# Two-level seven-product matrix multiplication: the last stage without GpSimd arithmetic, sums added by accumulating transfers

## The chip, the core and the metric

One core of one Trainium2 chip runs the kernel. The metric is the device time of the whole program in microseconds; the time of the kernel before is the median of three runs.

## The reference, cut to what matters

```python
X = np.fft.rfft(x, axis=1)                 # x: 8 x 3008 x 256, float32
Yr = Xr @ w_r - Xi @ w_i + b_r             # and Yi alike, then a soft threshold of 0.01
y = np.fft.irfft(Yr + 1j * Yi, n=3008, axis=1)

xt = y.transpose(0, 2, 1)
h = np.maximum(xt @ w_tok1, 0.0) @ w_tok2  # token mixing, 3008 -> 256 -> 3008
u = y + h.transpose(0, 2, 1)
h2 = np.maximum(u @ w_ch1, 0.0) @ w_ch2    # channel mixing, 256 -> 1536 -> 256
return u + h2
```

The last stage of the kernel computes the last two lines for units 2 to 4 (six of the eight batches): `u`, the two channel products with a ReLU between them, and `u + h2`.

## The kernel before, in words

The spectral part and the first two batches run first, up to about 1212 us of the span; the change leaves them alone. Then `channel7` takes over for the remaining tokens, in 17 chunks `n` of up to 1024 tokens. A chunk is cut into two halves of h = 512 tokens (448 or 490 in three of them), and the 256 channels into two blocks of 128, so `u` is a 2 x 2 block matrix `uf`. Both channel products are made with a seven-product scheme (P1 to P7 in place of eight block products). Every number is split into a high and a low part, so each product is three matmuls (`pinned`, line 1059): high x high, high x low, low x high.

`first7(n, g)` makes the hidden blocks of one group g (two groups of `TRIO` = 3 pairs of hidden blocks). For each pair it makes seven products into three PSUM banks: `x`, `w` and `q`. In order: P1 into x, copied by ScalarE (line 1076) to the block `c11`; P5 into w, copied to `c22` (1079); P6 added onto x, copied to `r12` (1082); P2 into q, added by VectorE to `c11` (1085); P7 added onto x, added by VectorE to `c22` (1088); P3 added onto w, added to `r12` by VectorE (1091), ReLU by ScalarE (1092); P4 added onto x, ReLU by ScalarE into `r21` (1095). The sequence P7, P3, P4 matters below: P4 adds into bank x, so it can't start until VectorE has read x after P7. The banks come from a pool of four.

`second7(n, g, ...)` makes the second channel product of group g, 21 products: results r = 0 to 6, three pairs k each, accumulated in one of three PSUM banks (`wc["sbanks"]`). `prepare(j, slot)` makes the moving operand of product j five steps ahead (`LEAD`): for r = 1, 2, 4, 6 VectorE first combines hidden blocks (lines 1122, 1124, 1126, 1128), then ScalarE makes the high part `rh` (1130 or 1133), then the low part `rl` is a subtraction: on VectorE for r = 0 and 5 (1131), and at line 1135 on GpSimd (`G`), but for three of the fifteen on VectorE. `product(j)` runs the three matmuls and fetches the weights of result r + 2 (`weights2`, line 1100, on SP's DMA queue, three buffers). When a result has its third pair, VectorE adds it to its block of `uf` (line 1147: seven such sums a group, r = 0 and r = 3 going to the same block); in the second group `store7` (line 1160) then stores finished blocks from SP's queue.

`channel7` interleaves them: one step is one first product and, from the second group on, `step()`: one second product of the group before, 21 steps behind, and one `prepare`. A step is thus six matmuls. Between steps stand the token mixing of the next chunk (`make_parts`, lines 1059 and 873, into bank `pu`; 37 sets of two halves), the block sums of its u (`sum_u`, lines 1037 to 1040) and its splits (`split_u7`, lines 150 and 153). TensorE's order is that of the program; the other queues are ordered ahead of time by a planner from its model of when each operand is ready, so an operation may stand earlier or later there than in the text. Every queue runs strictly in its order on the chip.

Of the kernel before, what the change touches and what calls it, by code (L numbers as in the profile page):

```python
# [11 lines left out]
F32 = mybir.dt.float32  # L12
F32R = mybir.dt.float32r
U32 = mybir.dt.uint32
AF = mybir.ActivationFunctionType
ALU = mybir.AluOpType
# [16 lines left out]
CW = 512  # L33
# [4 lines left out]
CW7 = 2 * CW  # L38
TRIO = 3
LEAD = 5  # L40
AT = (0, 3, 4, 1, 5, 6, 2)
SLOW = 1.75
SPECTRAL = 70.3 + NG * (SLOW - 0.7)
# [86 lines left out]
def tile_kernel(ctx: ExitStack, tc: tile.TileContext, io):  # L130
    nc = tc.nc
    V, S, G, PE, DMA, PUT = nc.vector, nc.scalar, nc.gpsimd, nc.tensor, nc.sync, nc.scalar
# [12 lines left out]
    def bank(name):  # L145
        return ps.tile([128, 512], F32, tag="w", name=name)
# [883 lines left out]
    def sum_u(n):  # L1030
        cw = chunks[n][2]
        h = cw // 2
        uf = ufs.pop(n)
        b11, b12, b21, b22 = (uf[:, t, k * h:(k + 1) * h] for t in range(2) for k in range(2))
        t = wc["seven"].tile([128, 4, CW], F32, tag="t7", name="t7", bufs=1)
        t1, t2, t3, t4_ = (t[:, k, :h] for k in range(4))
        V.tensor_tensor(out=t1, in0=b12, in1=b11, op=ALU.subtract)
        V.tensor_tensor(out=t2, in0=b22, in1=t1, op=ALU.subtract)
        V.tensor_tensor(out=t3, in0=b22, in1=b12, op=ALU.subtract)
        V.tensor_tensor(out=t4_, in0=b21, in1=t2, op=ALU.subtract)  # L1040
        us[n] = uf, (b11, t1, t2, b21, t3, b22, t4_), []

    def split_u7(n, i):
        h = chunks[n][2] // 2
# [12 lines left out]
    def pinned(out, wh, wl, xh, xl, start):  # L1057
        for n, (w, x) in enumerate(((wh, xh), (wh, xl), (wl, xh))):
            m = PE.matmul(out, lhsT=w, rhs=x, start=start and n == 0, stop=n == 2, skip_group_check=True)  # L1059
            tc.keep_in_program_order(m)  # L1060

    def first7(n, g):
        h = chunks[n][2] // 2
        ubs = us[n][2]
        blocks = [wc["tail"].tile([128, TRIO, CW], F32, tag="blk", name=k, bufs=8) for k in ("c11", "c22", "r12", "r21")]
        yield blocks
        for k in range(TRIO):
            p = TRIO * g + k
            c11, c22, r12, r21 = (t[:, k, :h] for t in blocks)
            x, w, q = (bank(name)[:, :h] for name in ("sx", "sw", "sq"))  # L1070

            def product(out, a, i, start):
                pinned(out, *left(p, a), ubs[i][:, 0, :h], ubs[i][:, 1, :h], start)

            product(x, 4, 0, True)
            S.copy(out=c11, in_=x)  # L1076
            yield
            product(w, 0, 1, True)
            S.copy(out=c22, in_=w)
            yield  # L1080
            product(x, 1, 2, False)
            S.copy(out=r12, in_=x)
            yield
            product(q, 5, 3, True)
            V.tensor_tensor(out=c11, in0=q, in1=c11, op=ALU.add)
            yield
            product(x, 2, 4, False)
            V.tensor_tensor(out=c22, in0=x, in1=c22, op=ALU.add)  # L1088
            yield
            product(w, 3, 5, False)  # L1090
            V.tensor_tensor(out=r12, in0=w, in1=r12, op=ALU.add)
            S.activation(out=r12, in_=r12, func=AF.Relu)
            yield
            product(x, 6, 6, False)
            S.activation(out=r21, in_=x, func=AF.Relu)
            yield

    def weights2(g, r):
        a = wc["seven"].tile([128, TRIO, 2, 128], F32R, name="a2s", bufs=3)
# [3 lines left out]
    def second7(n, g, blocks, odd):  # L1103
        h = chunks[n][2] // 2
        uf = us[n][0]
        banks = wc["sbanks"]
        x, w, q = (banks[i][:, :h] for i in ((2, 1, 0) if odd else (0, 1, 2)))
        outs = (x, w, x, q, x, w, x)
        homes = ((0, 0), (1, 1), (0, 1), (0, 0), (1, 1), (0, 1), (1, 0))
        weights, ready = {}, {}  # L1110

        def fetch(r):
            if r < 7:
                weights[r] = weights2(g, r)

        def prepare(j, slot):
            r, k = divmod(j, TRIO)
            hi, lo = (wc[name][:, slot, :h] for name in ("rh", "rl"))
            a, b, c, d = (t[:, k, :h] for t in blocks)
            src = (a, a, a, d, c, b, a)[r]  # L1120
            if r == 1:
                V.scalar_tensor_tensor(out=a, in0=a, scalar=0.0, in1=c, op0=ALU.max, op1=ALU.subtract)
            if r == 2:
                V.scalar_tensor_tensor(out=a, in0=b, scalar=0.0, in1=a, op0=ALU.max, op1=ALU.add)  # L1124
            if r == 4:
                V.scalar_tensor_tensor(out=c, in0=b, scalar=0.0, in1=c, op0=ALU.max, op1=ALU.subtract)
            if r == 6:
                V.tensor_tensor(out=a, in0=d, in1=a, op=ALU.subtract)  # L1128
            if r in (0, 5):
                S.activation(out=hi, in_=src, func=AF.Relu)  # L1130
                V.scalar_tensor_tensor(out=lo, in0=src, scalar=0.0, in1=hi.bitcast(F32), op0=ALU.max, op1=ALU.subtract)  # L1131
            else:
                S.copy(out=hi, in_=src)  # L1133
                eng = V if k == 0 and 2 <= r <= 4 else G
                eng.tensor_tensor(out=lo, in0=src, in1=hi.bitcast(F32), op=ALU.subtract)  # L1135
            ready[j] = hi, lo

        def product(j):
            r, k = divmod(j, TRIO)
            if k == 0:  # L1140
                fetch(r + 2)
            hi, lo = ready.pop(j)
            pinned(outs[r], weights[r][:, k, 0], weights[r][:, k, 1], hi, lo, r in (0, 1, 3) and k == 0)
            if k == TRIO - 1:
                i, j = homes[r]
                o = uf[:, i, j * h:(j + 1) * h]
                V.tensor_tensor(out=o, in0=outs[r], in1=o, op=ALU.add)  # L1147
                if g == 1 and r >= 3:
                    store7(n, i, j)

        return SimpleNamespace(prepare=prepare, product=product, fetch=fetch)

# [22 lines left out]
    def channel7(ns):  # L1175
        channels.close()
        wc["tail"] = ctx.enter_context(tc.tile_pool(name="tail", bufs=1, reuse_waits="tile"))
        for name, old in (("rh", "w2h"), ("rl", "w2l")):
            wc[name] = const.tile([128, 2 * TRIO, CW], F32R, tag=old, name=name)
        sums.close()  # L1180
        ps3 = ctx.enter_context(tc.tile_pool(name="ps3", bufs=1, space=bass.MemoryType.PSUM, reuse_waits="tile"))
        wc["sbanks"] = [ps3.tile([128, 512], F32, name=f"s{i}") for i in range(3)]
        wc["pu"] = ps3.tile([128, 512], F32, name="pu")
        seconds, count = [], [-7 * TRIO]

        def step():
            j = count[0]
            count[0] += 1
            if j >= 0:
                seconds[j // 21].product(j % 21)  # L1190
                if j % 21 in (19, 20) and j // 21 + 1 < len(seconds):
                    seconds[j // 21 + 1].fetch(j % 21 - 19)
            j += LEAD
            if 0 <= j < 21 * len(seconds):
                seconds[j // 21].prepare(j % 21, j % 6)

        for n in ns:
            after = n + 1 if n + 1 < len(chunks) else None
            mine = list(needs[after]) if after else []
            makes = {}  # L1200
            for i, g in enumerate(mine):
                m = make_parts(g)
                first = 1 + 6 * i if n == ns[0] else 22 - 9 * (len(mine) - 1 - i)
                makes[first], makes[first + (3 if n == ns[0] else 4)] = (m, i), (m, i)
            for g in range(2):
                f = first7(n, g)
                blocks = next(f)
                seconds.append(second7(n, g, blocks, len(seconds) % 2))
                if len(seconds) == 1:
                    for r in range(2):  # L1210
                        seconds[0].fetch(r)
                for t in range(7 * TRIO):
                    at = 7 * TRIO * g + t
                    next(f)
                    step()
                    if at in makes:
                        m, i = makes[at]
                        if next(m, None) is not None and i + 1 < len(mine):
                            load_wt2(mine[i + 1])
                            load_b2(mine[i + 1])  # L1220
                    if at == 33:
                        load_ahead(n + 2)
                    if after:
                        if at == 30:
                            sum_u(after)
                        if at in (32, 34):
                            split_u7(after, at // 2 - 16)
                        if at >= 37:
                            split_u7(after, at - 35)
        for _ in range(7 * TRIO):  # L1230
            step()

# [88 lines left out]
```

## Time and profile of the kernel before

| | us |
|---|---|
| median of three runs | 2477.83 (2476.95 to 2484.16) |
| the profiled execution | 2493.84 |
| its span, first to last instruction | 2492.1 |
| TensorE, busy | 2364.7 (95%) |
| VectorE, busy | 1843.5 (74%) |
| ScalarE, busy | 1336.6 (54%) |
| GpSimd, busy | 855.0 (34%) |

A busy time adds up the records of an engine's instructions. Records of neighbours overlap: matmuls are pipelined, and a VectorE or ScalarE instruction starts shortly before the one ahead of it has ended. So a busy share is not a share of the engine's own pace, and where pace matters the starts of neighbours are compared. The span has stages with different limits; the last one, from 1212 to 2488 us, is half of it.

### The profile page before, as it was taken

Reading aid. Unit: us, or ns where it says so; the run is one execution under the profiler, and the core shown is the slowest. Engines: PE = TensorE matmul, PEld = TensorE weight load, DVE = VectorE, ACT = ScalarE, POOL = GpSimd, SP = SyncE. Lnnn points to the kernel's source line nnn. Section 1 sums busy time; section 2 is a strip of 40 time slices with the busy share of each in tenths; the row PEclk is TensorE's granted clock in tenths of the full one; section 3 lists DMA queues with packets and bytes.
Section 4 is the critical chain, followed back from the end, with each engine's and each line's share of the span. In section 5 each row is a group of like instructions: output and inputs, shape, how many; then the busy total and the mean of one; then the engine's idle time right before and its main releaser. Section 6 shows DMA issues by size and latency. Waiting matters only on the chain.

```text
span 2492.1 us, 33718 instructions
## 1 busy us (share of the span) xinstructions
PE 2364.7 (95%) x12236; PEld 2032.4 (82%) x12236; DVE 1843.5 (74%) x2650; ACT 1336.6 (54%) x2419; POOL 855.0 (34%) x631
## 2 busy tenths in 40 slices
PE   8999999999999999999999999999999999998998
PEld 7778989999878888999787777887777778777776
DVE  7975667655656665554489888888888888988888
ACT  6754445444444443333466665666665566565665
POOL 0000332222222321221045444444444444444455
PEclk9999999999999999999999999999999999999998
DMA  8875577656466645434434444444444344453323
GB/s 213 259 239 168 161 238 216 184 168 195 139 193 185 179 147 190 142 119 135 153 114 127 129 146 135 135 136 125 136 127 143 111 132 132 130 162 114 117 89 97
DMA packets 196723, 383.73 MB, mean 154 GB/s; under 512 B 15893, under 2 KB 109677, under 8 KB 196557
## 3 DMA queue, kind: packets, MB, share of 16 engines
q1 hardware_dynamic: 162169, 314.98, 42.4%
q10 hardware_dynamic: 34388, 66.60, 8.0%
q8 instruction: 97, 1.59, 0.3%
q14 instruction: 69, 0.57, 0.1%
HBM read 274.30 MB, written 107.22 MB: 153 GB/s over the span
## 4 chain that ended last, share of the span: by engine, by line
PE 53%; DVE 30%; ACT 7%; DMA 4%; issue 3%; POOL 2%; SPq 1%; ACTq 0%; POOLq 0%; DVEq 0%
PE s L1059 6%; PE sx L1059 4%; DVE c L1124 4%; PE pu L873 3%; DVE rl L1131 3%; DVE c L1128 3%; PE ph L200 2%; PE px L488 2%; DVE ub L153 2%; PE po L201 2%; PE ph L202 2%; PE ph L201 2%; PE po L202 2%; DVE uf L1147 2%; PE po L200 2%
## 5 line engine op out<-in xcount | busy, mean ns | idle before, releaser
L1135 POOL TENSOR_TENSOR rl<-c,rh 128x512 fp32r<-128x512 f32 (+2 forms) x272 | 395.0, 1457 | 612.8 <-ACT rh L1133 523.6
L1059 PE MATMUL s<-rh,a2s 128*128 128x512 f32 (+2 forms) x1428 | 561.5, 396 | 0.1
L1059 PEld LDWEIGHTS s<-rh,a2s 128*128 128x128 f32 x1428 | 276.1, 193 | 56.7 <-ACT rh L1133 0.7
L1059 PE MATMUL s<-rl,a2s 128*128 128x512 f32 (+2 forms) x714 | 283.4, 397 | 5.6 <-POOL rl L1135 5.6
L1133 ACT CAST rh<-c 128x512 fp32r<-128x512 f32 (+2 forms) x306 | 187.2, 613 | 142.2 <-DVE c L1124 50.5
L1059 PE MATMUL sx<-ub,w 128*128 128x512 f32 (+2 forms) x612 | 193.8, 428 | 73.3 <-DVE c L1088 73.1
L1135 POOL TENSOR_TENSOR rl<-r,rh 128x512 fp32r<-128x512 f32 (+2 forms) x136 | 204.8, 1519 | 118.8 <-ACT rh L1133 109.5
L1059 PEld LDWEIGHTS sx<-ub,w 128*128 128x128 f32 x612 | 117.0, 203 | 116.9 <-DVE c L1088 97.8
L1131 DVE SCALAR_TENSOR_TENSOR rl<-c,rh 128x512 fp32r<-128x512 f32 (+2 forms) x204 | 165.4, 815 | 51.9 <-ACT rh L1130 51.5
L153 POOL TENSOR_TENSOR yl<-z,yh 128x512 fp32r<-128x512 f32 x72 | 96.1, 1335 | 301.9 <-ACT yh L150 301.8
L1147 DVE TENSOR_TENSOR uf<-s,uf 128x512 f32<-128x512 f32 (+2 forms) x238 | 159.5, 670 | 42.0 <-PE s L1059 42.0
L1059 PE MATMUL sx<-ub,ws 128*128 128x512 f32 (+2 forms) x612 | 177.1, 398 | 6.2 <-ACT c L1076 5.8
L914 DVE SCALAR_TENSOR_TENSOR hlo<-ph,hh 128x512 fp32r<-128x512 f32 (+4 forms) x180 | 113.9, 636 | 90.3 <-ACT hh L913 89.2
L913 ACT ACTIVATE hh<-ph 128x512 fp32r<-128x512 f32 (+4 forms) x180 | 100.1, 558 | 136.2 <-PE ph L202 131.4
L1130 ACT ACTIVATE rh<-c 128x512 fp32r<-128x512 f32 (+2 forms) x204 | 128.4, 630 | 82.6 <-PE s L1059 41.1
L1059 PE MATMUL sw<-ub,ws 128*128 128x512 f32 (+2 forms) x612 | 172.3, 390 | 0.0
L491 POOL TENSOR_TENSOR xf<-xf 128x256 f32<-128x256 f32 x84 | 72.9, 868 | 281.4 <-ACT xf L490 246.1
L1059 PEld LDWEIGHTS s<-rl,a2s 128*128 128x128 f32 x714 | 137.9, 193 | 36.2 <-POOL rl L1135 8.4
L153 DVE TENSOR_TENSOR xtl<-xf,xth 128x768 fp32r<-128x768 f32 x84 | 85.6, 1019 | 109.9 <-ACT xth L150 109.8
L200 PE MATMUL pm<-wmh,xth 128*128 128x256 f32 x504 | 146.3, 291 | 8.6 <-ACT xth L150 6.6
L201 PE MATMUL pm<-wml,xth 128*128 128x256 f32 x504 | 143.2, 284 | 0.0
L202 PE MATMUL pm<-wmh,xtl 128*128 128x256 f32 x504 | 143.0, 285 | 0.0
(185 smaller groups left out, 6171.5 us busy)
## 6 DMA issues: line engine op xcount, KB each, us to landing
a2s<-a_d SPq DMA_DIRECT2D x238, 384.0 KB, 3.0
wt<-wt_d SPq DMA_DIRECT2D x28, 940.0 KB, 5.8
x<-in_x SPq DMA_DIRECT2D x39, 480.0 KB, 4.6
wt<-ws_d SPq DMA_DIRECT2D x36, 512.0 KB, 3.7
a<-a_d SPq DMA_DIRECT2D x36, 512.0 KB, 5.0
b_d<-bt ACTq DMA_DIRECT2D x36, 512.0 KB, 4.7
a_d<-a ACTq DMA_DIRECT2D x36, 480.0 KB, 4.7
wt<-wt_d SPq DMA_DIRECT2D x21, 752.0 KB, 6.0
```

What stands on the lines that cost most here:

```text
L153: lo_eng.tensor_tensor(out=lo, in0=src, in1=hi.bitcast(F32), op=ALU.subtract)
L200: PE.matmul(out, lhsT=wh, rhs=xh, start=start, stop=False, skip_group_check=more)
L201: PE.matmul(out, lhsT=wh, rhs=xl, start=False, stop=False, skip_group_check=more)
L202: PE.matmul(out, lhsT=wl, rhs=xh, start=False, stop=stop, skip_group_check=more)
L913: S.activation(out=hh, in_=pt, func=AF.Relu)
L914: V.scalar_tensor_tensor(out=hlo, in0=pt, scalar=0.0, in1=hh.bitcast(F32), op0=ALU.max, op1=ALU.subtract)
L1059: m = PE.matmul(out, lhsT=w, rhs=x, start=start and n == 0, stop=n == 2, skip_group_check=True)
L1130: S.activation(out=hi, in_=src, func=AF.Relu)
L1131: V.scalar_tensor_tensor(out=lo, in0=src, scalar=0.0, in1=hi.bitcast(F32), op0=ALU.max, op1=ALU.subtract)
L1133: S.copy(out=hi, in_=src)
L1135: eng.tensor_tensor(out=lo, in0=src, in1=hi.bitcast(F32), op=ALU.subtract)
L1147: V.tensor_tensor(out=o, in0=outs[r], in1=o, op=ALU.add)
```

## The change

In the first products, P1 is copied by ScalarE from bank x into bank q (a bank of its own, `fq`, kept through the stage), P2 is accumulated onto it by TensorE, and ScalarE takes the ReLU of the sum straight into block `c11`: VectorE's addition of line 1085 is gone. So that TensorE adds onto what ScalarE wrote, `accumulator` runs one matmul over the bank at the start. The order becomes P1, P5, P4 of the pair before, P6, P2, P3, P7; P4 is thus deferred behind the next pair's P1 and P5. With `fq` kept, three banks of the pool are left for x and w. Blocks are tiles of one pair each, in 18 buffers.

In the second products, r = 0 is copied by ScalarE into the bank in which r = 3 then accumulates, so six sums a group are left. Each is copied by ScalarE to a staging tile (`st`, four buffers), and a DMA issued from GpSimd's queue adds it to the block of `uf` in SBUF (`accum_op`). All low parts are made by VectorE. The splits of the next chunk's u are one or two steps earlier in part.

```diff
+ADD = "dma"
...
-            product(x, 4, 0, True)
-            S.copy(out=c11, in_=x)
...
+            def p1():
+                nonlocal x
+                x = bank("sx")[:, :h]
+                product(x, p, 4, 0, True)
+                S.copy(out=q, in_=x)
...
+            def p2():
+                product(q, p, 5, 3, False)
+                S.activation(out=block(0, k), in_=q, func=AF.Relu)
...
+            def p7():
+                product(x, p, 2, 5, False)
+                c22 = blocks[1][k]
+                V.tensor_tensor(out=c22, in0=x, in1=c22, op=ALU.add)
+
+            def p4():
+                product(x, p, 6, 6, False)
+                S.activation(out=block(3, k), in_=x, func=AF.Relu)
+
+            return p1, p5, p4, p6, p2, p3, p7
...
-            if r in (0, 5):
+            if r == 5:
...
-                S.copy(out=hi, in_=src)
-                eng = V if k == 0 and 2 <= r <= 4 else G
-                eng.tensor_tensor(out=lo, in0=src, in1=hi.bitcast(F32), op=ALU.subtract)
+                split(hi, lo, src, S, V)
...
-                V.tensor_tensor(out=o, in0=outs[r], in1=o, op=ALU.add)
-                if g == 1 and r >= 3:
-                    store7(n, i, j)
+                if r == 0:
+                    S.copy(out=q, in_=x)
+                else:
+                    add(r)
+
+        def add(r):
+            i, j = homes[r]
+            o = uf[:, i, j * h:(j + 1) * h]
+            if ADD == "dma":
+                t = wc["tail"].tile([128, CW], F32, tag="st", name="st", bufs=4)[:, :h]
+                S.copy(out=t, in_=outs[r])
+                G.dma_start(out=o, in_=t, accum_op=ALU.add)
...
+            if g == 1 and r >= 3:
+                store7(n, i, j)
...
-                    next(f)
+                    k, i = divmod(t, 7)
+                    if i != 2:
+                        pairs[k][i]()
+                    elif last4:
+                        last4()
+                    if i == 2:
+                        last4 = pairs[k][2]
                     step()
```

## Rows read from the trace of the kernel before

**Rows 1.** Busy time by stretch, last stage: PE, PEld, DVE, ACT, POOL, clock, DMA, GB/s

```profile
1212.00:2488.00 1276.00, 1187.54 (x5404) 979.85 (x5402) 1086.35 (x1434) 770.54 (x1436) 597.02 (x408) 0.97 0.42 126
```

**Rows 2.** The products' line 1059: idle before it (us, times), by what ended it

```profile
  DVE c L1088: 171.0, 126
  ACT c L1076: 16.2, 22
  POOL rl L1135: 14.0, 14
```

**Rows 3.** Chain that ended last, in order of time: start, length in us, what

```profile
1214.19 1.03 PE pu L1059 x6
1215.22 0.88 PE pu L873 x8
...
1748.31 0.68 PE s L1059 x3
...
1750.35 1.28 PE pu L1059 x6
1751.63 1.09 PE pu L873 x10
```

**Rows 4.** Last stage by line and shape: count, busy us, mean ns, idle before

```profile
L1135 POOL TENSOR_TENSOR rl<-c,rh 128x512 fp32r<-128x512 f32 x224 | 330.9, 1482 | 448.1 <-ACT rh L1133 361.8 <-DVE c L1088 73.8 <-DVE r L1126 11.8
L1131 DVE SCALAR_TENSOR_TENSOR rl<-c,rh 128x512 fp32r<-128x512 f32 x168 | 135.7, 812 | 43.5 <-ACT rh L1130 43.1
L1124 DVE SCALAR_TENSOR_TENSOR c<-c,c 128x512 f32<-128x512 f32 x84 | 103.7, 1250 | 20.7 <-POOL rl L1135 20.7
L1128 DVE TENSOR_TENSOR c<-r,c 128x512 f32<-128x512 f32 x84 | 84.0, 1027 | 7.9 <-POOL rl L1135 7.9
L1126 DVE SCALAR_TENSOR_TENSOR r<-c,r 128x512 f32<-128x512 f32 x84 | 80.9, 990 | 0.1
L1085 DVE TENSOR_TENSOR c<-sq,c 128x512 f32<-128x512 f32 x84 | 57.1, 680 | 0.0
L1135 DVE TENSOR_TENSOR rl<-r,rh 128x512 fp32r<-128x512 f32 x56 | 52.2, 932 | 0.0
```

**Rows 5.** VectorE and GpSimd in order of time: start, length in us

```profile
1779.31 0.67 DVE L1131 SCALAR_TENSOR_TENSOR rl<-c,rh 128x512 fp32r<-128x512 f32 x1
1779.91 0.68 DVE L1088 TENSOR_TENSOR c<-sx,c 128x512 f32<-128x512 f32 x1
...
1781.63 1.30 POOL L1135 TENSOR_TENSOR rl<-c,rh 128x512 fp32r<-128x512 f32 x1 [3.40 <-ACT rh L1133]
...
1781.71 1.77 DVE L1131 SCALAR_TENSOR_TENSOR rl<-c,rh 128x512 fp32r<-128x512 f32 x1
```

**Rows 6.** ScalarE in order of time: first and last of twelve without a pause

```profile
1782.36 0.58 ACT L1095 ACTIVATE r<-sx 128x512 f32<-128x512 f32 x1
...
1787.90 0.64 ACT L150 CAST ub<-uf 128x512 fp32r<-128x512 f32 x1
```

**Rows 7.** Who waited for whom in the last stage: total us, times, longest

```profile
ACT r L1092 <- DVE r L1091: 128.6, 66, 4.0
...
DVE rl L1131 <- ACT rh L1130: 51.5, 49, 1.7
```

**Rows 8.** Stores (line 1160), then weight fetches (1100): issue ns, landing; SP's queue

```profile
L1160 SPq DMA_DIRECT2D out<-uf x74: 332/338/867, 1296.9 to 2489.1; - x74
DMA to landing us min/median/max: 1.4/2.6/6.5
...
L1100 SPq DMA_DIRECT2D a2s<-a_d x238: 319/320/542, 1193.2 to 2478.2; - x119
DMA to landing us min/median/max: 2.7/3.0/6.8
...
1775.22 38.61 SPq L1100 DMA_DIRECT2D a2s<-a_d  x9
```

**Rows 9.** The end of the chain: start, length in us, what

```profile
2483.08 3.21 POOL rl L1135 x2
...
2488.36 0.69 DVE uf L1147
```

More of the change, by code (lines that the diff above doesn't have):

```diff
@@ L1040, in sum_u @@
         V.tensor_tensor(out=t4_, in0=b21, in1=t2, op=ALU.subtract)
-        us[n] = uf, (b11, t1, t2, b21, t3, b22, t4_), []
+        us[n] = uf, (b11, t1, t2, b21, b22, t3, t4_), []
     def split_u7(n, i):
@@ L1060, in pinned, with accumulator @@
             tc.keep_in_program_order(m)
+    def accumulator(t):
+        w = wc["w1"][:, 0, 0]
+        tc.keep_in_program_order(PE.matmul(t, lhsT=w[:, :128], rhs=w[:, :CW], start=True, stop=True))
     def first7(n, g):
@@ L1064, in first7 @@
         ubs = us[n][2]
-        blocks = [wc["tail"].tile([128, TRIO, CW], F32, tag="blk", name=k, bufs=8) for k in ("c11", "c22", "r12", "r21")]
-        yield blocks
-        for k in range(TRIO):
-            p = TRIO * g + k
[L1069 to L1073, printed above, removed]
-            product(x, 4, 0, True)
-            S.copy(out=c11, in_=x)
[L1077 to L1096, printed above, removed]
@@ new lines, in first7, with block, product, pair @@
+        blocks = [[None] * TRIO for _ in range(4)]
+        steps = []
+        def block(i, k):
+            blocks[i][k] = wc["tail"].tile([128, CW], F32, tag="blk", name=("c11", "c22", "r12", "r21")[i], bufs=18)[:, :h]
+            return blocks[i][k]
+        def product(out, p, a, i, start):
+            pinned(out, *left(p, a), ubs[i][:, 0, :h], ubs[i][:, 1, :h], start)
+        def pair(k):
+            p = TRIO * g + k
+            x, w = None, None
+            q = wc["fq"][:, :h]
+            def p1():
[3 more added lines that the diff above has]
+                S.copy(out=q, in_=x)
+            def p5():
+                nonlocal w
+                w = bank("sw")[:, :h]
+                product(w, p, 0, 1, True)
+                S.copy(out=block(1, k), in_=w)
+            def p6():
+                product(x, p, 1, 2, False)
+                S.copy(out=block(2, k), in_=x)
+            def p2():
+                product(q, p, 5, 3, False)
+                S.activation(out=block(0, k), in_=q, func=AF.Relu)
+            def p3():
+                product(w, p, 3, 4, False)
+                r12 = blocks[2][k]
+                V.tensor_tensor(out=r12, in0=w, in1=r12, op=ALU.add)
+                S.activation(out=r12, in_=r12, func=AF.Relu)
+            def p7():
[6 more added lines that the diff above has]
+            return p1, p5, p4, p6, p2, p3, p7
@@ L1098, in weights2 @@
+        return [pair(k) for k in range(TRIO)], blocks
     def weights2(g, r):
@@ L1106, in second7 @@
         banks = wc["sbanks"]
-        x, w, q = (banks[i][:, :h] for i in ((2, 1, 0) if odd else (0, 1, 2)))
+        x, w = (t[:, :h] for t in (banks[:2], banks[1::-1])[odd])
+        q = banks[2][:, :h]
         outs = (x, w, x, q, x, w, x)
-        homes = ((0, 0), (1, 1), (0, 1), (0, 0), (1, 1), (0, 1), (1, 0))
+        homes = (None, (1, 1), (0, 1), (0, 0), (1, 1), (0, 1), (1, 0))
         weights, ready = {}, {}
@@ L1118, in prepare @@
             hi, lo = (wc[name][:, slot, :h] for name in ("rh", "rl"))
-            a, b, c, d = (t[:, k, :h] for t in blocks)
+            a, b, c, d = (t[k] for t in blocks)
             src = (a, a, a, d, c, b, a)[r]
             if r == 1:
-                V.scalar_tensor_tensor(out=a, in0=a, scalar=0.0, in1=c, op0=ALU.max, op1=ALU.subtract)
+                V.tensor_tensor(out=a, in0=a, in1=c, op=ALU.subtract)
             if r == 2:
@@ L1142, in product @@
             hi, lo = ready.pop(j)
-            pinned(outs[r], weights[r][:, k, 0], weights[r][:, k, 1], hi, lo, r in (0, 1, 3) and k == 0)
+            pinned(outs[r], weights[r][:, k, 0], weights[r][:, k, 1], hi, lo, r < 2 and k == 0)
             if k == TRIO - 1:
-                i, j = homes[r]
-                o = uf[:, i, j * h:(j + 1) * h]
+                if r == 0:
[9 more added lines that the diff above has]
+                G.dma_start(out=o, in_=t, accum_op=ALU.add)
+            else:
                 V.tensor_tensor(out=o, in0=outs[r], in1=o, op=ALU.add)
-                if g == 1 and r >= 3:
-                    store7(n, i, j)
+            if g == 1 and r >= 3:
+                store7(n, i, j)
         return SimpleNamespace(prepare=prepare, product=product, fetch=fetch)
@@ L1183, in channel7 @@
         wc["pu"] = ps3.tile([128, 512], F32, name="pu")
+        wc["fq"] = bank("fq")
+        accumulator(wc["fq"])
         seconds, count = [], [-7 * TRIO]
@@ L1187, in step @@
             j = count[0]
+            if j == 0:
+                accumulator(wc["sbanks"][2])
             count[0] += 1
@@ L1195, in step @@
                 seconds[j // 21].prepare(j % 21, j % 6)
+        last4 = None
         for n in ns:
@@ L1205, in channel7 @@
             for g in range(2):
-                f = first7(n, g)
-                blocks = next(f)
+                pairs, blocks = first7(n, g)
                 seconds.append(second7(n, g, blocks, len(seconds) % 2))
@@ L1227, in channel7 @@
                             split_u7(after, at // 2 - 16)
-                        if at >= 37:
-                            split_u7(after, at - 35)
+                        if at in (36, 37, 39, 40, 41):
+                            split_u7(after, {36: 2, 37: 3, 39: 4, 40: 5, 41: 6}[at])
+        last4()
         for _ in range(7 * TRIO):
```

## The prediction

> **What bounds the kernel now.** I looked at the last stage alone, since the diff touches nothing before it. First the busy time by stretch [rows 1]: the stage lasts 1276 us, TensorE is busy nearly throughout, VectorE for 1086 us, ScalarE for 771, GpSimd for 597, and the granted TensorE clock is 0.97. A busy TensorE here is not one at its own pace, so next I took that pace from the chain of work that ended last [rows 3]: three 512-wide matmuls take 0.68 us, 0.227 each; half a set of parts takes 1.28 + 1.09 = 2.37 us with five slots and 1.03 + 0.88 = 1.91 with four. The stage has 17 chunks x 2 groups x 42 products x 3 = 4284 matmuls: 3528 of 512 columns, 504 of 448, 252 of 490. At 0.227 us, scaled by width, that is 801 + 100 + 55 = 956 us. The 37 sets of parts, two halves each, are 40 x 2.37 + 34 x 1.91 = 160. **TensorE needs 1116 us of the 1276; 160 us are waiting**, the lower clock that follows it included.
>
> Then the waits at the products' line [rows 2]: 171 us of idle time end with VectorE's line 1088, 16 with ScalarE's 1076, 14 with GpSimd. (The list counts matmuls and weight loads, so I use it as shares: with the smaller entries it comes to some 217 us, and line 1088 is 171/217 of it, 126 of the 160 us.) Line 1088 reads bank x after P7; P4, the second product behind it, adds into the same bank. The bank is late because VectorE is: its queue carries contention. Alone, a two-input operation takes 680 ns, as line 1085 does, and starts 0.60 us after the one before it; but lines 1124, 1128, 1126, 1131 and 1135 average 1250, 1027, 990, 812 and 932 ns [rows 4]. Single records show why: the operation of 1781.71 us takes 1.77 us beside a GpSimd subtraction of 1.30 that began at 1781.63 [rows 5]. Over 84, 84, 84, 168 and 56 operations the excess is 48 + 29 + 26 + 22 + 14 = 139 us of VectorE time.
>
> **The change part by part.**
> *GpSimd's 408 subtractions go to VectorE.* Per group VectorE has now 9 additions in the first products, 12 combinations, 9 low parts and 7 sums into u, 37 operations; with 11 per chunk to split u (16 chunks) that is 34 x 37 + 176 = 1434, the count of [rows 1]. After: 6 + 12 + 21 + 0 = 39 a group, 34 x 39 + 176 = 1502. At a pitch of 0.60 us [rows 5] and 0.983 for the narrower chunks: 846 us before, plus at least the 139 of contention; 886 us after, without it. So VectorE does more operations in less time, if nothing else holds it up: 79% of TensorE's 1116.
>
> *P1 by ScalarE into P2's bank, sums copied out by ScalarE.* Per group it gains 3 operations in the first products (six a pair for five) and 7 copies of sums: +10, 34 x 10 on top of 1436 [rows 1] = 1776. Twelve ScalarE operations in a row start from 1782.36 to 1787.90 us [rows 6], 11 steps of 0.504. 1776 x 0.504 x 0.983 = 880 us, also 79%. A copy from PSUM to PSUM is not in the trace; I price it as the copies to SBUF; at double it would add 51 us to ScalarE, still below TensorE.
>
> *Pairs overlapped.* P4 now stands behind the next pair's P1 and P5, so between P7 and P4 lie two steps in place of one; a step is two products, 1.36 us. The waits for line 1088 are 171 us in 126 cases, 1.36 us each [rows 2]: the new gap is as long as the mean wait. Waits spread around that mean would leave about a third, 45 us of 126; VectorE's queue, shorter by 139 us of contention, should lower that. I take 25 us, ends 0 and 126. P6 and P7 gain a step too, so the wait for line 1076 should go; in exchange only three banks rotate for x and w, and ScalarE is fuller. For these other waits, 34 us now, I take 25, ends 0 and 60. The two matmuls that set up accumulation cost half a microsecond in all.
>
> *Sums by accumulating transfers.* 34 x 6 = 204 transfers of 256 KB from the GpSimd queue. The trace has no such transfer, and none issued there. Nearest rows: a store of at most 256 KB takes 0.34 us to issue and lands after 2.6 us in the median, 6.5 at most [rows 8]; GpSimd's own operation takes 1.48 [rows 4]. In the middle of the stage I cost them at nothing. What hides them: GpSimd has nothing else; a group's six transfers have 33 us; the four staging buffers give each one four sums' time, 4 x 4.07 = 16.3 us, before ScalarE's queue, with everything for later products behind it, would stand on it. The Trainium skill (DMA: Bandwidth & Descriptors, Anatomy of one DMA) gives about 2.0 us plus bytes/436e3 for a transfer from this queue, an estimate of 2.6 us here; by that price too the cover holds, and no row here can show it.
>
> *Stores behind the sums.* On SP's queue a store now waits for a landing, not for VectorE, and weight fetches are queued behind it. Fetches are issued as a weight buffer falls free, nine in 38.6 us [rows 8], two results (8.1 us) before use, and land after 3.0 us. That leaves 5.1 us; a store that holds SP up to 6.5 us after a result costs a fetch due 4.07 us after it 2.4. I take nothing; without the cover, 68 stores x 1.4 us (6.5 less 5.1) = 95 us.
>
> *The end.* The last sum was one VectorE operation of 0.69 us [rows 9]; it becomes a copy, a transfer (2.6 to 6.5) and then the store: +3 to +6. The last GpSimd pair, 3.21 us [rows 9], becomes two VectorE operations of 0.6: -2. I take +2.
>
> **Sum.** 1116 + 25 + 25 = 1166 against 1276: -110, +2 = -108 us. On the profiled execution (2493.8, span 2492.1) that gives 2386; its ratio to the median of the runs, 2477.83, is 0.994, so on the median about **2370 us**. With the ends of the two waits alone: 2478 - 158 = 2320 and 2478 + 26 = 2504.
>
> **The rivals.**
> *A. VectorE and ScalarE wait for each other (2440 us).* In 12 of 21 steps the high part needs VectorE's combination, and the low part, now always VectorE's, needs the high part: 0.68 + 0.62 + 0.60 and some 0.1 of hand-over, 2.0 us against TensorE's 1.36. If VectorE's queue stood at each, a group would take 12 x 2.0 + 9 x 1.36 = 36.2 us, 34 x 36.2 x 0.983 = 1210; the 160 us of parts, in which the two engines catch up only partly, bring it to about 1235: -41. For it: VectorE waited 51.5 us for ScalarE at line 1131 already [rows 7], and ScalarE 128.6 for line 1091. Against it: only 49 of 204 low parts waited; the others found other work in front of them. The change not doing what it says ends here as well: if GpSimd's issuing blocks VectorE as its subtractions did, by 1.1 us [rows 5] for each of 204 transfers, VectorE has 886 + 224 = 1110 us of work, TensorE's whole time.
>
> *B. The transfers crowd out the weights (2475 us).* The stage moves 126 GB/s at a share of 0.42 [rows 1], 300 GB/s when full. An accumulation reads twice and writes once: at worst 3 x 0.87 = 2.6 us of all engines, 204 x 2.6 = 535 us beside the present 0.42 x 1276 = 536: 92% of 1166. Were a fetch then to land after 8.1 us in place of 3.0, the gain would be eaten. Against it: the longest today is 6.8 [rows 8], and TensorE waited for none. The Trainium skill (the same page, Issuing engines are not separate DMA queues) says that transfers from all queues share 16 engines and interleave, which is the rule behind this rival; no run yet shows how an accumulation shares them.
>
> *C. The accumulations are taken one at a time and become the bound (2558 us, slower).* The point from which this decides is the stage's time per sum: (1276 - 30)/204 = 6.1 us, the 30 us being the first group before any sum. At 6.5 us each, the longest landing of a store [rows 8], the stage is 204 x 6.5 + 30 = 1356: +80. For it: one queue in order, a form that this trace does not have. Against it: 2.6 us is the median, and nothing needs one transfer to wait for another but a second one to the same block, nine steps later.
>
> **How the numbers follow.** Forecast 0.63, A 0.17, B 0.08, C 0.12. The range goes from 2330 (nearly no waits left) past A to 2480 (B): 0.12 of C and a little below are left out. Measurements of this kernel can tell about 0.3%, 7 us: faster 0.80 (forecast and A), same 0.08 (B), slower 0.12 (C).
>
> **What would show it.** Right: no operation of GpSimd in the stage but issues; lines of two-input VectorE work at 0.68 us, none at 1.78; TensorE's idle time at bank x under a third of the 171 us; the stage at about 1166 us with VectorE and ScalarE near 80% and the clock above 0.97. Wrong: VectorE low parts that mostly wait for ScalarE (A), matmuls that wait for weights (B), ScalarE's staging copy waiting for a transfer (C), or many new waits for ScalarE's copies at the banks of the second products.

## The result, and the profile after

| | median, us | ratio to before, 95% interval |
|---|---|---|
| before, four runs | 2480.99 | |
| changed kernel, four runs | 2395.23 | 0.9646 [0.9605, 0.9687] |

The change makes the kernel 3.5% faster. The profiled execution has a span of 2398.2 us for 2492.1: 94 us less, where 108 were forecast.

Busy time by stretch, last stage of the changed kernel, with the columns of [rows 1]:

```profile
1212.00:2394.00 1182.00, 1148.04 (x5411) 972.03 (x5409) 927.78 (x1503) 940.95 (x1776) 177.22 (x204) 0.98 0.71 181
```

The counts are those of the forecast (1502 and 1776; one of VectorE's belongs to the stage ahead). In this view a stretch in which two records of an engine overlap counts once. That a busy time adds the records up, as the section on the kernel before says, is wrong here: 1503 records of some 0.68 us would add up to over 1000 us. VectorE is busy for 928 us in place of 1086 with 68 operations more, and GpSimd's 177 us are the issues of 204 transfers, 0.86 us each. TensorE's products run from 1213.9 to 2390.0 us, 1176 us, of which 1116 are its work by the sum of the prediction.

What TensorE waited for at the products' line, now 1061 (us, times), which answers to [rows 2]; then at line 875, the matmuls on b2, the token mixing's spectral blocks:

```profile
  DMA wt<-wt_d: 8.3, 7
  ACT rh L152: 6.9, 7
...
  DVE c L1115: 1.4, 2
...
  DMA b<-b_d: 44.1, 33
```

The wait for VectorE at bank x (line 1115 is the old 1088) is gone: 1.4 us for 171. In its place stands a wait that the kernel before hardly had (1.0 us in three cases): 44 us for the load of b2. The queues show where that comes from. SP's queue, who waited for whom (total us, times, longest), then the chain of work around one such wait (start, length):

```profile
SPq L1127 <- PE s L1061: 662.2, 206, 10.5
SPq L1197 <- DMA uf<-st: 307.4, 67, 7.1
...
1851.05 5.82 DMA uf<-st
1856.86 0.02 issue
1856.88 0.33 SPq L1197
1857.21 0.04 issue
1857.26 0.02 SPq L849
1857.27 0.34 issue
1857.61 5.56 DMA b<-b_d
1863.17 0.04 issue
1863.21 1.88 PE pu L875 x8
```

An accumulating transfer lands, the store that waited for it at the head of SP's queue goes out, the load of b2 behind the store goes out 0.4 us after the store's issue ends, and TensorE stands until it lands. The buffer of b2 had been free since 1851.92, 5.7 us before the load went out (the last matmuls on the old contents):

```profile
1850.89 1.03 PE L875 MATMUL pu<-g,b 96*128 96x94 f32 x8
```

The stage loads b2 36 times. In the changed kernel 17 of these loads were issued more than 3 us after the last matmul on the old contents, in the kernel before 2.

VectorE's operations by shape answer to [rows 4]:

```profile
L155 DVE TENSOR_TENSOR rl<-c,rh 128x512 fp32r<-128x512 f32 x336 | 226.0, 687 | 96.4 <-ACT rh L152 78.6 <-PE sx L1061 8.0 <-PE sw L1061 3.2
...
L1152 DVE SCALAR_TENSOR_TENSOR c<-c,c 128x512 f32<-128x512 f32 x84 | 55.2, 684 | 0.0
```

Line 1152 is the old 1124: 684 ns for 1250.

### The profile page after: what moved, and what is told of

It is laid out like the page before. It is cut to its first block, busy times and chain, and to the rows that moved or that the text cites. A ratio compares the mean times of both kernels' runs of the same rounds, so it can differ in the third digit from the quotient of the medians.

```text
span 2398.2 us, 34177 instructions
## 1 busy us (share of the span) xinstructions
PE 2323.3 (97%) x12238; PEld 2023.1 (84%) x12238; DVE 1683.9 (70%) x2718; ACT 1506.2 (63%) x2759; POOL 435.6 (18%) x427
## 3 DMA queue, kind: packets, MB, share of 16 engines
q1 hardware_dynamic: 162169, 314.98, 43.8%
## 4 chain that ended last, share of the span: by engine, by line
PE 80%; DMA 9%; DVE 5%; issue 3%; ACT 1%; POOL 1%; SPq 1%; POOLq 0%; ACTq 0%; DVEq 0%
PE s L1061 18%; PE sx L1061 11%; PE sw L1061 5%; PE pu L875 5%; DMA b<-b_d 3%; PE pu L1061 3%; PE fq L1061 3%; PE po L203 3%; PE px L490 3%; PE ph L202 3%; PE po L204 3%; PE po L202 2%; PE ph L203 2%; PE ph L204 2%; PE pm L202 2%
## 5 line engine op out<-in xcount | busy, mean ns | idle before, releaser
L1061 PE MATMUL s<-rh,a2s 128*128 128x512 f32 (+2 forms) x1428 | 553.3, 390 | 1.9 <-DMA a2s<-a_d 1.9
L1182 POOL DMA_DIRECT2D uf<-st x204 | 177.2, 869 | 1057.3 <-ACT st L1181 862.1
L155 DVE TENSOR_TENSOR rl<-c,rh 128x512 fp32r<-128x512 f32 (+2 forms) x408 | 270.9, 678 | 112.6 <-ACT rh L152 92.4
L152 ACT CAST rh<-c 128x512 fp32r<-128x512 f32 (+2 forms) x408 | 244.3, 622 | 28.4 <-PE s L1061 21.2
L884 ACT COPY uf<-pu 128x470 f32<-128x470 f32 (+16 forms) x152 | 61.7, 425 | 202.1 <-PE pu L875 192.0
L1061 PE MATMUL sx<-ub,w 128*128 128x512 f32 (+2 forms) x612 | 177.4, 399 | 0.5 <-DVE c L1115 0.5
L875 PEld LDWEIGHTS pu<-g,b 96*128 96x128 f32 x1024 | 134.7, 198 | 28.3 <-DMA b<-b_d 25.1
L875 PE MATMUL pu<-g,b 96*128 96x94 f32 x1024 | 136.3, 280 | 19.0 <-DMA b<-b_d 19.0
L155 DVE TENSOR_TENSOR rl<-r,rh 128x512 fp32r<-128x512 f32 (+2 forms) x204 | 135.2, 677 | 19.9 <-ACT rh L152 19.5
L202 PE MATMUL ph<-uh,w 128*128 128x512 f32 (+4 forms) x360 | 138.3, 385 | 3.7 <-DVE hlo L916 3.0
```

The source lines that it names most:

```text
L155: lo_eng.tensor_tensor(out=lo, in0=src, in1=hi.bitcast(F32), op=ALU.subtract)
L202: PE.matmul(out, lhsT=wh, rhs=xh, start=start, stop=False, skip_group_check=more)
L875: m = PE.matmul(pt[:, s * TOKS:(s + 1) * TOKS], lhsT=b2[:, s, cs], rhs=g2[:, 0 if s0 + s == 0 else 1], start=False, stop=s == k - 1, skip_ ...
L884: S.copy(out=ufs[m][:, ct, lo - at:hi - at], in_=pt[:, lo - c0:hi - c0])
L1182: G.dma_start(out=o, in_=t, accum_op=ALU.add)
```

## The experiments

Theory 1: the loss of the kernel before was GpSimd's subtractions slowing VectorE's two-input operations, and what is left after the change is SP's queue behind stores that wait for accumulations. Rivals: the overlap of the pairs did it; VectorE's lighter load did it; and, for what is left, the accumulations' share of the DMA engines. Every edit also lets the planner order the queues anew, so no run holds the order fixed; where that matters it is said.

| kernel | median, us | ratio to before, 95% interval |
|---|---|---|
| after2 | 2389.11 | 0.9627 [0.9591, 0.9663] |
| stores_gpsimd | 2406.60 | 0.9692 [0.9657, 0.9727] |
| add_vector | 2353.99 | 0.9489 [0.9468, 0.9511] |
| no_overlap | 2388.97 | 0.9631 [0.9608, 0.9654] |
| sum_scratch | 2351.43 | 0.9482 [0.9460, 0.9505] |
| low_gpsimd | 2520.85 | 1.0161 [1.0136, 1.0186] |
| before_low_vector | 2388.57 | 0.9634 [0.9617, 0.9652] |
| vector_no_overlap | 2358.83 | 0.9511 [0.9491, 0.9531] |
| dummy_gpsimd | 2618.01 | 1.0542 [1.0524, 1.0560] |
| vector_low_gpsimd | 2483.32 | 1.0009 [0.9996, 1.0022] |
| mixed | 2352.96 | 0.9482 [0.9467, 0.9498] |

### after2: the changed kernel beside the others

No edit.

> The changed kernel once more, unaltered, so that the others of this group have it beside them on the same chip. All theories: 0.965 of the kernel before, about 2395 us, with 25 us of TensorE time above its pace ahead of line 875 (the matmuls on b2) in the last stage.

As expected: 0.9627, and the waits for b2 come to 43.8 us. The two measurements of the changed kernel, 2395 and 2389 us, are what the others are held against.

### stores_gpsimd: the stores in another queue

```diff
-                DMA.dma_start(out=outv[bi][:, i:i + 1, ...], in_=uf[:, i:i + 1, ...])
+                G.dma_start(out=outv[bi][:, i:i + 1, ...], in_=uf[:, i:i + 1, ...])
```

> The stores of the last stage are issued from GpSimd's queue in place of SP's; all else as in the changed kernel. Theory 1 (a store on SP's queue waits for the accumulating transfer, 310 us in 68 cases, and holds the load of b2 queued behind it): the b2 loads go out as soon as the buffer is free, TensorE's 44 us of listed waiting for b2 fall under 10, and the time falls by 20 to 25 us, to about 2372. Rival (the loads land late because the accumulations share the 16 DMA engines): the waits for b2 stay at 30 us or more and the time stays within 7 us of 2395. If GpSimd's queue, which then waits for each landing before the next accumulation, held up ScalarE's staging copy, the time would be above 2400 and the staging copy would show waits for a transfer.

A miss: 2407 us. Waits for b2 fell from 44 to 29 us only, and others came (who waited for whom, total us, times, longest):

```profile
POOL out L1197 <- DMA uf<-st: 274.2, 62, 9.5
...
PEld pu L1061 <- ACT uf L884: 14.3, 11, 3.9
...
PE pu L1061 <- ACT uf L884: 9.8, 9, 3.5
...
ACT uf L884 <- DMA out<-uf: 44.4, 11, 5.7
```

The store's wait did not go away, it moved: GpSimd's queue stands 274 us behind landings, the stores land later, and ScalarE's copy of the next u into the same buffer waits 44 us for them (10 in the changed kernel). So the time of this run does not separate the two theories; sum_scratch does. ScalarE's staging copy, the place at which I had looked for trouble, waited for no transfer. The load of b2 was no longer held in SP's queue: 2 of 36 went out more than 3 us late, for 17. It still cost 29 us because it landed later, 7.9 us (480 KB) and 8.7 us (384 KB) after its issue in the median, for 7.3 and 7.2 in add_vector. Why it landed later stays open.

### add_vector: the sums by VectorE again

```diff
-ADD = "dma"
+ADD = "vector"
```

> The sums of the last stage are added into u by VectorE as in the kernel before, with no staging copy and no accumulating transfer; all else as in the changed kernel. VectorE gets 204 operations more (886 + 120 = 1006 us of the stage's 1127 us of TensorE work), ScalarE 204 fewer. Theory 1: the stores wait for VectorE alone, the waits for b2 fall under 10 us, VectorE at 90% costs some of it back: 2375 to 2395, so the accumulations bought nothing. Rival (moving the sums off VectorE is what the gain rests on): VectorE becomes late again at the banks, 2420 or more.

2354 us, better than either end of what theory 1 had said and 35 us better than the changed kernel. The stage (columns as above) and the waits:

```profile
1212.00:2351.00 1139.00, 1127.52 (x5393) 956.55 (x5391) 1040.78 (x1705) 848.44 (x1571) 0.00 (x0) 1.00 0.47 141
...
PEld sx L1061 <- DVE c L1115: 1.1, 1, 1.1
...
PEld pu L875 <- DMA b<-b_d: 2.8, 7, 0.7
```

VectorE at 1041 us of 1139 makes nobody wait: 1.8 us at bank x, weight loads and matmuls together. The granted clock is 1.00. The accumulating transfers, meant to relieve VectorE, cost 35 us together with the stores that wait for them and the staging copies; sum_scratch below takes them apart.

### no_overlap: P4 right behind its own pair

```diff
-            return p1, p5, p4, p6, p2, p3, p7
+            return p1, p5, p6, p2, p7, p3, p4
...
-                    if i != 2:
-                        pairs[k][i]()
-                    elif last4:
-                        last4()
-                    if i == 2:
-                        last4 = pairs[k][2]
+                    pairs[k][i]()
...
-        last4()
```

> The pairs are not overlapped: the order is P1, P5, P6, P2, P7, P3, P4 within each pair, so one step stands between P7 and P4 as in the kernel before; all else as in the changed kernel. Theory 1 (VectorE was late at bank x because of GpSimd's subtractions beside it): the bank is free in time for the most part, 5 to 20 us more than the changed kernel, 2400 to 2415. Rival (the added step is what removed the wait): the wait for VectorE at bank x returns with 80 us or more, 2455 to 2480.

2389 us: no difference. TensorE waits 2.6 us for VectorE at bank x with one step between P7 and P4, as in the kernel before. The overlap is not needed for the wait to go.

### sum_scratch: the same transfers, nobody waiting for them

```diff
-                G.dma_start(out=o, in_=t, accum_op=ALU.add)
+                wc["ns"] = wc.get("ns", -1) + 1
+                G.dma_start(out=wc["scratch"][wc["ns"] % 4][:, :h], in_=t, accum_op=ALU.add)
...
+        wc["scratch"] = [wc["tail"].tile([128, CW], F32, name=f"sums{i}") for i in range(4)]
...
```

> The accumulating transfers are issued as in the changed kernel, same size, queue and number, but into four scratch tiles in place of u, so the stores do not wait for them; the sums are thereby left out of u. Theory 1 (stores that wait on SP's queue hold the load of b2 behind them): the waits for b2 fall from 44 us to under 10 and the time falls by 20 to 25 us, to about 2368. Rival (the accumulations slow the loads by sharing the DMA engines): b2 lands later than with VectorE's sums (7.3 us), the waits for it stay at 25 us or more, the time within 8 us of 2390.

2351 us, 38 below the changed kernel and level with add_vector, with all 204 transfers in place. Issues and landings (KB, median us), and the waits for b2:

```profile
sums<-st POOLq DMA_DIRECT2D x168, 256.0 KB, 3.7
...
b<-b_d SPq DMA_DIRECT2D x20, 480.0 KB, 7.6
...
PEld pu L875 <- DMA b<-b_d: 2.4, 6, 0.6
...
PE pu L875 <- DMA b<-b_d: 0.5, 2, 0.3
```

The DMA engines carry as much as in the changed kernel (a share of 0.72 for 0.71), b2 lands after 7.6 us for 7.3 in add_vector, and the wait for it is 2.9 us. So it was not the traffic. The run does more than its edit says: with no sum to wait for, the planner sends each store earlier (the first at 1187 us for 1296), where it waits for ScalarE's copies of u, and none stands directly ahead of a load of b2, as one does for 15 of 36 loads in the changed kernel. That a store costs only where it waits for a landing is seen from the kernel before: 13 of its loads stand directly behind a store, the stores wait for VectorE, and b2 cost it 1.0 us. The gain of 38 exceeds the 20 to 25 expected. The listed waits for b2 fall by 41 us, so nearly all of them count, where the expectation took about half; the granted clock is 1.00 for 0.98.

### low_gpsimd: the low parts back on GpSimd

```diff
-                split(hi, lo, src, S, V)
+                split(hi, lo, src, S, V if r == 0 or k == 0 and 2 <= r <= 4 else G)
```

> Twelve of the 21 low parts of a group go back to GpSimd, as in the kernel before; all else as in the changed kernel (VectorE 1094 operations, fewer than before and after). Theory 1 (GpSimd's subtractions beside VectorE's two-input operations were the loss): those operations average 800 to 1250 ns again, the chain of low parts through GpSimd is late, and most of the gain is lost: 2430 to 2470. Rival (the gain came from fewer VectorE operations and the new order, not from GpSimd's silence): with 408 operations fewer on VectorE the time stays at 2400 or falls.

2521 us: with everything else of the change in place, the kernel is 41 us, 1.6%, slower than before, beyond the expected end. Lines 1152 and 1156 (the old 1124 and 1128) average 1065 and 1025 ns again. What TensorE waited for at the products' line:

```profile
  DVE r L1109: 130.0, 67
  DVE c L1115: 34.0, 23
```

With the overlap and under contention, the wait at bank x is 34 us for 171, but 130 us stand at bank w, which line 1109 (the old 1091) reads after P3 and where the kernel before waited for nothing; only three banks rotate now. So the wait moved and nothing was gained. Which part of the change moves it was not tried apart.

### before_low_vector: one edit to the kernel before

```diff
-                eng = V if k == 0 and 2 <= r <= 4 else G
-                eng.tensor_tensor(out=lo, in0=src, in1=hi.bitcast(F32), op=ALU.subtract)
+                V.tensor_tensor(out=lo, in0=src, in1=hi.bitcast(F32), op=ALU.subtract)
```

> The kernel before with one edit: all low parts on VectorE, GpSimd idle in the last stage. VectorE then has 1842 operations, 1086 us at its pace beside TensorE's 1127. Theory 1: without contention even that fits nearly, and the time falls to 2385 to 2430. Rival (VectorE needs the 9 operations a group that the change takes from it): VectorE at 96% is late at every bank, 2460 or more.

2389 us: one line gives what the whole change gives. VectorE is busy for 1113 us of 1170, and it shows a little. The stage, line 1124 as it is without GpSimd beside it, and the waits at bank x:

```profile
1212.00:2382.00 1170.00, 1136.92 (x5365) 952.83 (x5363) 1112.72 (x1838) 786.55 (x1430) 0.00 (x0) 1.00 0.45 137
...
L1124 DVE SCALAR_TENSOR_TENSOR c<-c,c 128x512 f32<-128x512 f32 x84 | 56.5, 682 | 0.0
...
PEld sx L1059 <- DVE c L1088: 38.8, 38, 3.0
PE sx L1059 <- DVE c L1088: 23.1, 24, 2.6
```

62 us of listed waits at bank x for 171 before, with 408 operations more on VectorE. At its 0.605 us an operation (1112.72/1838) the 1434 operations of the kernel before would be busy for 868 us; they were for 1086. The 218 us between are 0.53 for each of GpSimd's 408 subtractions.

### vector_no_overlap: no transfers and no overlap

The edits of add_vector and no_overlap together.

> Sums by VectorE (no accumulating transfers) and pairs not overlapped: of the change are left the low parts on VectorE, P1 carried into P2's bank and r = 0 into r = 3's. Theory 1 (overlap buys nothing once GpSimd is silent): 2350 to 2362, as with the overlap. Rival (with VectorE at 89% the bank x is late again and the overlap earns its place): 2375 or more, with waits for VectorE at bank x of 20 us or more.

2359 us, in theory 1's range. TensorE waits 4.2 us for VectorE at bank x. Against before_low_vector it differs by the two carries (P1 into P2's bank, r = 0 into r = 3's), four VectorE operations a group, and by the blocks in tiles of their own and the earlier splits: 30 us together. Against add_vector it differs by the overlap: 5 us, and the intervals meet.

### dummy_gpsimd: subtractions that nobody reads

```diff
                 split(hi, lo, src, S, V)
+                if not (r == 0 or k == 0 and 2 <= r <= 4):
+                    G.tensor_tensor(out=wc["idle"][1][:, :h], in0=wc["idle"][0][:, :h], in1=hi.bitcast(F32), op=ALU.subtract)
...
+        wc["idle"] = [wc["tail"].tile([128, CW], F32, name=f"idle{i}") for i in range(2)]
...
```

> The kernel with VectorE's sums (add_vector), and beside it 408 subtractions on GpSimd whose result nobody reads: 12 a group, each on the high part just made, into a tile of its own. Nothing in the kernel waits for them but the reuse of that high part's buffer six steps later. Theory 1 (GpSimd's subtractions slow VectorE's two-input operations beside them): these average 750 to 1250 ns, VectorE's 1006 us grow by 130 us or more to above TensorE's 1127, and the time rises by 60 us or more from 2354, to 2415 to 2500. Rival (what cost time was the low part arriving 1.4 us late from GpSimd, not the contention): 2354 to 2370.

2618 us, 264 above add_vector, for work that is on nobody's path: no engine's wait is listed for these subtractions. The stage, and VectorE by line and shape:

```profile
1212.00:2614.00 1402.00, 1214.27 (x5399) 985.84 (x5397) 1374.14 (x1708) 835.53 (x1572) 640.21 (x408) 0.96 0.37 115
...
L155 DVE TENSOR_TENSOR rl<-c,rh 128x512 fp32r<-128x512 f32 x336 | 374.8, 1133 | 6.6 <-ACT rh L152 6.1
...
L1186 DVE TENSOR_TENSOR uf<-s,uf 128x512 f32<-128x512 f32 x168 | 114.1, 679 | 2.5 <-PE s L1061 2.5
...
L1150 DVE TENSOR_TENSOR c<-c,r 128x512 f32<-128x512 f32 x84 | 73.1, 872 | 0.9
...
L1115 DVE TENSOR_TENSOR c<-sx,c 128x512 f32<-128x512 f32 x84 | 57.0, 679 | 0.0
```

VectorE's busy time grows from 1041 to 1374 us: 333 us for 408 subtractions, 0.82 each. Operations that read two SBUF tiles pay (1133, 872 ns; line 1152 alone hardly, 694); those with one input in PSUM, lines 1186 and 1115, keep their 679 ns. The Trainium skill (SBUF — State Buffer, Who interferes with whom) draws that line: a VectorE instruction with two SBUF inputs contends with a GpSimd instruction that reads SBUF, one with at most one SBUF input and outside the two-port modes does not. This trace agrees.

### vector_low_gpsimd: less on VectorE, and slower

The edits of add_vector and low_gpsimd together.

> The kernel with VectorE's sums (add_vector), with twelve of the 21 low parts of a group given back to GpSimd; GpSimd issues no transfers. VectorE has 33 operations a group, 1298 in all, 766 us at its pace: fewer than in any other kernel here. Theory 1: contention and the chain through GpSimd make it slower than add_vector by 60 us or more all the same, 2415 to 2490; against the run with accumulations and GpSimd's low parts (2521) it shows what their sharing of GpSimd's queue cost, 30 us or more. Rival (VectorE's own load decides): 2354 or less.

2483 us, the kernel before to within 0.2%, though VectorE has 1298 operations where before has 1434. In the stage it is busy for 1027 us, 0.79 an operation against 0.61 in add_vector. Relieving VectorE by GpSimd gives back nothing, and with GpSimd's subtractions kept the carries and the overlap of the change gain nothing either. Against low_gpsimd the transfers, their copies and the waiting stores cost 38 us, and TensorE waits 66 us for b2 there and 3.5 here. They cost 35 without the subtractions (add_vector against after2), so nothing shows that subtractions and transfers hinder each other in GpSimd's queue.

### mixed: accumulations where no store follows

```diff
-            if ADD == "dma":
+            if ADD == "dma" and not (g == 1 and r >= 3):
```

> Accumulating transfers only for the eight sums of a chunk that no store follows; the four that a store follows are added by VectorE. Theory 1 (the accumulations cost time only where a store on SP's queue waits for one): no store waits for a transfer, the waits for b2 stay under 10 us, VectorE has 1570 operations: 2345 to 2358, level with add_vector. Rival (accumulations cost time by themselves, on GpSimd's or the DMA engines' side): 2370 to 2385, between add_vector and the changed kernel.

2353 us, in theory 1's range. Stores wait for VectorE (48 us in 63 cases), none for a transfer, and the weight loads at line 875 wait 3.4 us for b2. Two of the 36 loads of b2 go out more than 3 us late, as in add_vector, for 17 in the changed kernel. With add_vector and sum_scratch, at 2354 and 2351, it is the fastest here; of the kernels that compute the reference, add_vector and mixed beat the changed one by 35 and 36 us, and add_vector is the simpler.

## Why the prediction was right, and where it was not

**What bounded the kernel: right.** 171 us at line 1088 went to 1.4, and contention was the cause: before_low_vector edits nothing else and gains 3.7%, dummy_gpsimd adds nothing else and loses 11% on add_vector. The size was too low: the prediction counted 139 us on five lines' excess, as a lower bound, and before_low_vector puts it at 218. Its own sum showed this, 846 + 139 = 985 us against 1086 busy; line 1122, the splits at line 153 and 28 operations of line 1135 were left out. In dummy_gpsimd a subtraction costs more, 0.82 us for 0.53.

**VectorE's and ScalarE's sums: right.** Forecast 886 and 880 us at a pitch; the counts are 1502 and 1776, and no engine but TensorE became the bound. They were busy for 928 and 941 us, 5 and 7% above the forecast. The copies from PSUM to PSUM were priced as copies to SBUF, and that holds: 570 and 587 ns in the median (lines 1090 and 1172) for 581 at line 1076. The 51 us for a double price left out the 34 copies of r = 0; with them it would be 69.

**Pairs overlapped: the step failed.** The prediction let the added step carry most of the wait at bank x and then took off 25 us as left over. no_overlap and vector_no_overlap put the overlap at 0 and 5 us. The mean wait of 1.36 us that it set against a step belonged to a VectorE under contention; without contention there is no wait to shorten, and under contention the wait moves to bank w (low_gpsimd).

**Sums by accumulating transfers, stores behind the sums: the steps that cost the difference.** The first was priced at nothing, and of the transfers themselves that holds: sum_scratch loses nothing by them. The second was priced at nothing too, because a fetch of weights behind a store has 5.1 us to spare. That cover held: TensorE waited 3.5 us for weights. But weights are not all that is queued there: the load of b2 has one buffer, some 8 us between the buffer's release and its use, and 7.3 us to land (both in add_vector), and it stood behind the same stores. I had looked at one victim of the queue and not listed the others. A store waits 4.6 us (307/67), TensorE's listed waits for b2 are 44 us, and what goes when no store waits is 35 to 38.

**Waits 25 + 25 us: near in sum by luck.** Bank x was given 25 and took 1.4; the other waits were given 25 and took the rest of 60 (1176 less 1116), most of it for b2, which the prediction did not have. Two errors of 24 and 34 us in opposite directions brought the stage to 1176 for 1166.

**The end: +4 for +2.** From the last product to the span's end it takes 8 us for 4 before: a copy, an issue of 0.86, a landing of 3.8 in the median, and then the store.

**The sum.** -110 + 2 was forecast on the profiled execution; measured -99 (1275 to 1176 us between the first and the last product) and +4, and the stage begins 1 us later: -94. On the medians it is -86 in the first measurement and -95 in the second. (The upper end of the two waits, 2504, leaves out the +2 that the lower end has; it should read 2506.)

**The rivals.** A did not come: VectorE's low parts wait 112 us for ScalarE, and TensorE 0.8 for them. Nor did GpSimd's issuing hold VectorE up, at 684 to 689 ns. B's rule, the Trainium skill's sentence that transfers of all queues share 16 engines and interleave (DMA: Bandwidth & Descriptors, Issuing engines are not separate DMA queues), agrees with the share, 0.71 for 0.42, and costs nothing here: weights land after 3.1 us for 3.0. An accumulation keeps the 16 engines busy for about 1.5 us, an estimate from the shares of this kernel and add_vector ((0.71 x 1182 - 0.47 x 1139)/204), between the 0.87 of a plain transfer and the 2.6 that B took at worst. C did not come: accumulations land after 3.8 us in the median, 8.9 at most, for 5.8 us of stage per sum. (The formula that the prediction cites gives 2.6; the measured landing decides.) Whether two of them move data at the same time is not shown.

Where the 3.5% comes from, on the medians: low parts to VectorE -91 us (before_low_vector), the two carries -30 (vector_no_overlap), the overlap -5 or nothing, the accumulating transfers with stores behind them +35 to +41. The shares hold in this order only: without the first, the next two are worth nothing (vector_low_gpsimd).

## What to carry to other kernels

Before giving GpSimd a share of VectorE's work, price what each of its operations does to VectorE's operations with two SBUF inputs: here 0.5 us each in the kernel before and 0.8 in dummy_gpsimd, where VectorE needs 0.6 to do the work itself. When a wait in an in-order queue grows, list everything that is queued behind it, with the time each has between its issue and its use; here the load with a single buffer paid. And a change of several parts that gains is worth taking apart: one line of it alone gave as much as the whole, and one part took 35 us back.

## What the runs showed of the hardware that I had not expected

An accumulating SBUF-to-SBUF transfer of 256 KB takes GpSimd 0.86 us to issue and lands after 3.8 us in the median; 204 of them do not slow VectorE's two-input operations. GpSimd subtractions off everybody's path lengthen a stage of 1139 us by 263. A queue's wait moved from SP to GpSimd came back as a wait for a buffer on ScalarE.
